# Issuing a decode kernel's V and up loads on a second queue

## The chip, the cores and the metric

The kernel runs on one core of one Trainium2 chip. The metric is the device time of one launch in microseconds (us). Most executions of a kernel lie close together, and some fall in a slow state: of the control's six times (c0_before, the kernel before with one comment changed) five are 440.16 to 440.79 us, within 0.15%, and one is 447.77 us, 1.7% longer. A ratio is the mean time of one kernel's fast runs over the mean time of the fast runs of the kernel before in the same rounds, on the same chip, so it is not quite the ratio of the medians that are quoted.

Abbreviations in the profile: PE is the matmul engine, DVE the vector engine, ACT the scalar engine, SP the engine that otherwise only issues transfers. SPq and ACTq are the queues on which those two engines issue DMA transfers; the text also calls such a queue a ring. L428 is line 428 of the kernel.

## The reference

One decode step of a transformer block with 8 sequences and one new token each: adaptive layer norm, grouped-query attention over a cache of 8192 positions, adaptive layer norm, gated MLP.

```python
mod = (silu(c) @ w_mod).reshape(8, 6, 1, -1)          # w_mod 1024 x 6144
h = layernorm(x) * (1 + ca) + sa
q = (h @ wq)                                          # wq 1024 x 4096, 32 heads of 128
scores = einsum('bhqd,bhkd->bhqk', q, k) * 128**-0.5  # k, v: 8 x 4 x 8192 x 128 bf16, 8 query heads per kv head
x = x + ga * (softmax(scores) @ v) @ wo               # wo 4096 x 1024
h = layernorm(x) * (1 + cb) + sb
x = x + gb * ((relu(h @ W_gate) * (h @ W_up)) @ W_down)   # 1024 x 3584, 1024 x 3584, 3584 x 1024
```

K and V are 67 MB each and the weights 51 MB. All 185.6 MB are read once.

## The kernel before

All large loads go through one list. An arena in SBUF is used as a ring, and a load is issued as soon as all readers of the bytes that it overwrites have been put in the program. Each load covers all 128 partitions.

```python
def load(key, src, n):
    stream.append((key, src, n))

def pump():                        # called after every operation that is recorded
    while stream:
        key, src, n = stream[0]
        lo = cursor[0] if cursor[0] + n <= RING else 0
        if P.unread("arena", lo, lo + n):
            return                 # the buffer still has readers to come
        stream.pop(0)
        cursor[0] = lo + n
        place[key] = lo
        dst = arena[:, lo:lo + n]
        # ... a view for 3-D sources ...
        P.op("sp", lambda e, dst=dst, src=src: e.dma_start(dst, src),
             writes=[slot_r(lo, lo + n)], dma=True)

# the order of the list (sizes in MiB):
#   wm0 6, wm1 6, wq0 4, wq1 4, K0 4, V0 4, K1 4, V1 4, ... K15 4, V15 4,
#   wo0 4, wo1 4, gate0 3.5, up0 3.5, gate1 3.5, up1 3.5, wd0 3.5, 1.75, 1, 0.5, 0.25
```

During attention the arena holds four buffers of 4 MiB: two for K and two for V. K(m+2) is issued when the last transpose of K(m) has ended, and V(m+2) when PV(m) has ended. One step m of attention is a chain over three engines:

```python
for m in range(16):
    for e8 in range(8):
        kt_part(m, e8)        # DVE: transpose an eighth of K(m)            L428
        qk_part(m, e8)        # PE: scores                                  L439
    rowmax; spread; headmax   # DVE, PE, DVE
    expo(m)                   # ACT: exp                                    L466
    p_turn(m)                 # DVE: transpose the probabilities            L473
    pv(m)                     # PE: probabilities times V(m), 32 matmuls    L482
```

The transposes of K(m+1) run while PV(m) runs. In this kernel each engine works off its own list of operations in order, and semaphores order the lists against one another.

## Time and profile before

| | |
|---|---|
| time, three runs | 439.91, 440.66 and 446.92 us, median 440.66 |
| bytes read | 185.6 MB |
| load queue's share of the 16 DMA engines | 98.4% |
| packet of 32 KB on one engine, from 100 us on | 1213 ns, which is 27.0 GB/s, and 432 GB/s for 16 engines |
| the profiled run | 445.6 us span, slow state |

These are lines of the page of the kernel before. The first two are rows of 40 equal slices of the span: the busy share of the DMA engines in tenths, and the rate. Then come the two queues that carry data, the chain that ended last, the group of K transposes with its idle time and what ended it, and the issue-to-landing times.

```profile
DMA  8999999999999999999999999999999999999994
GB/s 353 427 388 384 379 379 403 390 424 447 434 429 429 425 444 435 426 432 427 439 434 429 435 425 438 435 429 431 429 434 439 432 429 426 436 429 431 435 419 194
...
q1 hardware_dynamic: 6896, 185.64, 98.4%
...
q10 hardware_dynamic: 32, 0.01, 0.0%
...
DMA 48%; DVE 25%; PE 23%; ACT 2%; issue 1%; SPq 0%
...
L428 DVE STREAM_TRANSPOSE kt<-arena 128x1024 uint32<-128x1024 uint32 x128 | 148.6, 1215 | 44.6 <-DMA arena<-in_A_k_cache_dram 41.8
...
arena<-in_A_k_cache_dram SPq DMA_DIRECT2D x16, 4096.0 KB, 28.9
arena<-in_A_v_cache_dram SPq DMA_DIRECT2D x16, 4096.0 KB, 25.7
```

The engines are busy in every slice but the first and the last. The rate is flat near 430 GB/s from the ninth slice on. Queue q1 (SP) carries everything. K transposes wait 41.8 us in all for K, so compute keeps up with the loads. A load takes about 29 us from issue to landing although 4.19 MB at 432 GB/s are only 9.7 us: about two other loads are queued ahead of it.

The low rate of the third to eighth slice (379 to 403 GB/s) belongs to the slow state: in the three slow profiles packets took about 1355 instead of 1213 ns per 32 KB from about 20 us until 85 to 96 us into the run. The same kernel, run again as a control with one comment changed, fell in the fast state (438.4 us span), and its rate is flat from the second slice on (416 to 443 GB/s until the 38th). Below are its rates, the chain that ended last, the K transposes and the issue-to-landing time of K. The last two lines are from its timeline (start, duration, and in brackets how long the engine sat idle before and for whom): the first transpose of K0 and the last PV.

```profile
GB/s 359 434 416 438 437 443 432 431 431 429 434 431 431 429 431 434 430 434 431 431 432 434 434 435 443 434 434 429 434 429 431 434 429 431 431 433 431 432 420 195
...
PE 39%; DVE 29%; DMA 24%; ACT 4%; issue 2%; SPq 0%
...
L428 DVE STREAM_TRANSPOSE kt<-arena 128x1024 uint32<-128x1024 uint32 x128 | 149.1, 1215 | 40.3 <-DMA arena<-in_A_k_cache_dram 33.8 <-PE ps L439 6.4
...
arena<-in_A_k_cache_dram SPq DMA_DIRECT2D x16, 4096.0 KB, 28.5
...
62.90 6.88 DVE L428 STREAM_TRANSPOSE kt<-arena 128x1024 uint32<-128x1024 uint32 x6 [3.15 <-DMA arena<-in_A_k_cache_dram]
...
372.36 6.36 PE L482 MATMUL ps<-arena,pT 128*64 128x512 bf16 x32 [1.82 <-DVE pT L473]
```

So in the fast state compute on K0 starts at 62.9 us. This control is what the changed kernel, whose profile is fast too, is compared with.

### The profile page before, as it was taken

What the parts mean: (1) busy time and instruction counts of PE and PEld (TensorE: products, weight loads), DVE (VectorE), ACT (ScalarE), POOL (GpSimd) and SP (SyncE); (2) the same over time, 40 slices, a digit from 0 to 9 for tenths busy, and PEclk for the clock granted to TensorE, in tenths of its full rate; (3) what the DMA queues carried; (4) which work ended last, traced back from release to release, by engine and by line L of the source; (5) the groups of instructions that cost most, each with busy time, mean ns of one, the idle gap of its engine ahead of it and who ended that gap; (6) DMA issues with size and microseconds to landing.
All of it is one profiled execution on the core that took longest, in us unless ns stands there. A gap on an engine that the chain in (4) does not pass through costs nothing.

```text
span 445.6 us, 4024 instructions
## 1 busy us (share of the span) xinstructions
PE 273.7 (61%) x1691; PEld 121.9 (27%) x1691; DVE 262.9 (59%) x372; ACT 28.8 (6%) x48; POOL 19.9 (4%) x77
## 2 busy tenths in 40 slices
PE   0054347585775959577595867769595875564235
PEld 0021112222332423333242333324233332351112
DVE  0233028396878769687885967788686878521020
ACT  1100010201001010110101011010101001100000
POOL 6000010000000000000000000000000000000000
PEclk9997557796969789696987969688796988867555
DMA  8999999999999999999999999999999999999994
GB/s 353 427 388 384 379 379 403 390 424 447 434 429 429 425 444 435 426 432 427 439 434 429 435 425 438 435 429 431 429 434 439 432 429 426 436 429 431 435 419 194
DMA packets 6946, 185.90 MB, mean 417 GB/s; under 512 B 816, under 2 KB 912, under 8 KB 1168
## 3 DMA queue, kind: packets, MB, share of 16 engines
q1 hardware_dynamic: 6896, 185.64, 98.4%
q8 instruction: 13, 0.21, 0.2%
q14 instruction: 5, 0.04, 0.0%
q10 hardware_dynamic: 32, 0.01, 0.0%
HBM read 185.63 MB, written 0.02 MB: 417 GB/s over the span
## 4 chain that ended last, share of the span: by engine, by line
DMA 48%; DVE 25%; PE 23%; ACT 2%; issue 1%; SPq 0%
DMA arena<-in_A_k_cache_dram 33%; DVE kt L428 14%; PE ps L482 11%; DMA arena<-in_B_W_down_dram 8%; PE ps L439 8%; DMA arena<-in_w_mod_dram 7%; DVE pT L473 4%; DVE negm L446 3%; ACT prb L466 2%; PE ps L571 1%; PE ps L352 1%; PE ps L452 1%; PE ps L592 1%; DVE mj L457 1%; DVE kt L561 0%
## 5 line engine op out<-in xcount | busy, mean ns | idle before, releaser
L428 DVE STREAM_TRANSPOSE kt<-arena 128x1024 uint32<-128x1024 uint32 x128 | 148.6, 1215 | 44.6 <-DMA arena<-in_A_k_cache_dram 41.8
L439 PE MATMUL ps<-kt,qpad 128*128 128x512 bf16 x512 | 121.7, 382 | 12.7 <-DVE kt L428 10.8
L482 PE MATMUL ps<-arena,pT 128*64 128x512 bf16 x512 | 92.1, 539 | 50.5 <-DVE pT L473 50.5
L482 PEld LDWEIGHTS ps<-arena,pT 128*64 128x64 bf16 x512 | 44.3, 153 | 92.9 <-issue 87.3
L439 PEld LDWEIGHTS ps<-kt,qpad 128*128 128x128 bf16 x512 | 45.1, 97 | 87.8 <-DVE kt L428 32.3
L473 DVE STREAM_TRANSPOSE pT<-prb 64x1024 bf16<-64x1024 bf16 x32 | 39.6, 1239 | 15.9 <-ACT prb L466 15.4
L466 ACT ACTIVATE prb<-ps,bias 128x1024 bf16<-128x1024 f32 x16 | 17.8, 1114 | 276.3 <-DVE mjt L460 276.3
L446 DVE TENSOR_REDUCE negm<-ps 128x1 f32<-128x512 f32 x32 | 22.0, 686 | 10.7 <-PE ps L439 10.5
L421 POOL COPY qpad<-qR 32x32 bf16<-32x32 bf16 x64 | 13.1, 204 | 314.0 <-PE ps L439 255.4
L592 PE MATMUL ps<-arena,hT 128*32 128x448 bf16 x128 | 11.2, 522 | 15.9 <-DMA arena<-in_B_W_gate_dram 6.8
L452 PE MATMUL ps<-identf,negm 128*128 128x128 f32 x32 | 7.8, 325 | 15.7 <-DVE negm L450 15.7
L495 DVE SCALAR_TENSOR_TENSOR om<-ps,im,om 128x128 f32<-128x128 f32 x48 | 16.7, 348 | 0.6
L375 PE MATMUL ps<-arena,hT 128*32 128x512 bf16 x64 | 7.2, 631 | 14.7 <-DMA arena<-in_A_wq_dram 14.7
L599 DVE TENSOR_TENSOR kt<-ps,kt 128x448 bf16<-128x448 f32 x2 | 1.2, 620 | 25.0 <-PE ps L592 25.0
L500 PE MATMUL ps<-jmp,om 128*128 128x16 f32 x32 | 6.5, 280 | 14.7 <-DVE om L495 14.7
L290 DVE CAST cxr<-ps 128x512 bf16<-128x512 f32 x1 | 0.7, 692 | 19.2 <-PE ps L288 19.2
L288 PE MATMUL ps<-cx,rsel 32*128 32x512 bf16 x1 | 0.6, 581 | 18.6 <-DMA cx<-in_A_x_dram 18.6
L385 DVE CAST kt<-ps 128x512 bf16<-128x512 f32 x1 | 0.7, 693 | 18.3 <-PE ps L375 18.3
L610 PE MATMUL ps<-arena,kt 128*32 128x256 bf16 x112 | 6.9, 416 | 7.4 <-DMA arena<-in_B_W_down_dram 7.3
L452 PEld LDWEIGHTS ps<-identf,negm 128*128 128x128 f32 x32 | 4.7, 187 | 23.6 <-DVE negm L450 22.1
L352 PE MATMUL ps<-arena,hT 128*32 128x512 bf16 x96 | 9.0, 553 | 2.4 <-DMA arena<-in_w_mod_dram 2.4
L592 PEld LDWEIGHTS ps<-arena,hT 128*32 128x32 bf16 x128 | 4.2, 129 | 22.2 <-DMA arena<-in_B_W_up_dram 8.3
(80 smaller groups left out, 95.7 us busy)
## 6 DMA issues: line engine op xcount, KB each, us to landing
arena<-in_A_k_cache_dram SPq DMA_DIRECT2D x16, 4096.0 KB, 28.9
arena<-in_A_v_cache_dram SPq DMA_DIRECT2D x16, 4096.0 KB, 25.7
arena<-in_w_mod_dram SPq DMA_DIRECT2D x2, 6144.0 KB, 17.4
arena<-in_A_wq_dram SPq DMA_DIRECT2D x2, 4096.0 KB, 25.0
arena<-in_A_wo_dram SPq DMA_DIRECT2D x2, 4096.0 KB, 27.5
arena<-in_B_W_gate_dram SPq DMA_DIRECT2D x2, 3584.0 KB, 30.5
arena<-in_B_W_up_dram SPq DMA_DIRECT2D x2, 3584.0 KB, 33.5
arena<-in_B_W_down_dram SPq DMA_DIRECT2D x1, 3584.0 KB, 36.1
```

Source lines behind the costliest of these rows:

```text
L352: fns.append(lambda e, w=w, pr=pr, j=j, kk=kk: e.matmul(ps[32 * j:32 * j + 32, pr, :], hT[:, kk, :], w[:, 2 * pr:2 * pr + 2, j, :], start= ...
L375: fns.append(lambda e, w=w, z=z, g=g, kk=kk: e.matmul(ps[32 * g:32 * g + 32, 3 + z, :], hT[:, kk, :], w[:, g, z, :], start=(kk == 0), stop ...
L421: P.op("pool", lambda e, n=2 * m + Q // 2, Q=Q: e.tensor_copy(qpad[32 * Q:32 * Q + 32, m % 2, :, 24 + 32 * Q:32 + 32 * Q], qR[32 * Q:32 * ...
L428: P.op("dve", lambda e: e.transpose(ktb[:, to:to + QE].bitcast(dt.uint32), arena[:, lo:lo + QE].bitcast(dt.uint32)), reads=[slot_r(lo, lo ...
L439: fns.append(lambda e, t=t, r=r: e.matmul(ps[:, b, :].rearrange("p (c k) -> p c k", k=32), qpad[:, m % 2, t * 2 + r, 24 - 8 * i:152 - 8 * ...
L446: P.op("dve", lambda e: e.tensor_reduce(negm[:, h:h + 1], ps[:, b, :], AX.X, ALU.max, negate=True), reads=[bank(b)], writes=[R("negm", h, ...
L452: P.op("pe", lambda e: e.matmul(ps[:, 4, 0:128], negm[:, 2:3].to_broadcast([128, 128]), identf[:], start=True, stop=True), reads=[R("negm" ...
L466: P.op("act", lambda e: e.activation(prb[:], ps[:, 2 * z:2 * z + 2, :].rearrange("p h n -> p (h n)"), ACT.Exp, bias=bias[:, z:z + 1], scal ...
L473: P.op("dve", lambda e, g=g: e.transpose(pT[64 * g:64 * g + 64, z, :, g, :], prb[64 * g:64 * g + 64, :]), reads=[R("prb"), R("pT", z, z + ...
L482: fns.append(lambda e, t=t: e.matmul(ps[64 * (t % 2):64 * (t % 2) + 64, 5, :].rearrange("p (i d) -> p i d", d=Dh), pT[:, z, t].rearrange(" ...
L495: P.op("dve", lambda e, i=i: e.scalar_tensor_tensor(out=om[:], in0=ps[:, 5, Dh * i:Dh * i + Dh], scalar=im[:, i:i + 1], in1=om[:], op0=ALU ...
L592: fns.append(lambda e, w=w, r=kk - r0, kk=kk, h=h, j=j, b0=b0: e.matmul(ps[32 * j:32 * j + 32, b0 + h, 0:H], hT[:, kk, :], w[:, r, j, h, : ...
```

## The change

The intent: V and up loads are issued on ACT's queue, the rest on SP's, so that two rings feed every DMA engine at once.

```diff
-                P.op("sp", lambda e, dst=dst, src=src: e.dma_start(dst, src), writes=[slot_r(lo, lo + n)], dma=True)
+                P.op("act" if key[0] in ("v", "up") else "sp", lambda e, dst=dst, src=src: e.dma_start(dst, src), writes=[slot_r(lo, lo + n)], dma=True)
```

Buffers, sizes and the order of the list stay. Sixteen V loads and two up loads move to ACT's program, each at the place where it becomes legal.

## The prediction

> **What bounds it now.** The DMA stream. The queue table gives the single load queue 98.4% of 16 engines' span for 185.6 MB, and the 40-slice row shows nines almost throughout. In 5 us windows from 85 to 435 us the rate averages about 431 GB/s, and packet records there are 1213 ns per 32 KB packet, 27 GB/s per engine, 432 GB/s for 16. [...] 185.6 MB at 432 GB/s is 430 us; about 3 us before the first byte lands and 5 to 6 us from the last landing to the end make about 439, the fast time. The profiled run (445.6 us) was a slow one: until about 85 us its packets took some 12% longer (about 1355 ns per 32 KB), worth about 9 us.
>
> **Almost as tight: the compute chain.** In the chain of waits, stretches with no DMA in them repeat every 18.7 to 20.2 us per pair of loads (PV alone 4.9 to 6.6 us). Two 4.19 MB loads take 19.4 us.
>
> **What the change does.** It removes nothing: SP issues (0.33 us each) overlap transfers. It moves 16 V and 2 up issues to ACT, some 6 us in all (28.8 us busy, 276 us waiting before exp). Each V issue waits there for the PV that frees its slot, but the next exp comes after that PV anyway. The same bytes go through the same 16 engines, already at their limit. [...]
>
> What does change is order. V0 is issued at 39.4 us with wq0's rest, wq1 and K0 still queued; on its own ring it no longer waits behind them but takes half the engines [...]. My estimate from the transfer times: V0 lands about 12 us earlier, where nobody needs it, wq1 about 9 us and K0 about 13 us later, so the first K transpose, at 68.1 us now, starts about 13 us later and the compute chain stays late until the end. Does the DMA run dry? Queued ahead of a new K are about 19 us (28.9 to land less its own 9.7), ahead of a new V 16 us: enough for 13 us, barely. If the chain keeps 19.4 us per step, no idle; at 20 us per step the queue empties for some microseconds. At the end, wd's issue has about 24 us of queue ahead, so the tail hides the delay.
>
> **Prediction: 441.5 us, 438 to 449 in 8 of 10.** Faster by over 2%: 0.02; within 2%: 0.88; slower by over 2%: 0.10.
>
> **Signs.** Two load queues in the table, together 97 to 98%; GB/s still about 430 in the middle. K from issue to landing falls from 28.9 to about 16 us, V similar, because less is queued. DVE idle before the first K transpose grows by about 13 us; the last PV ends about 13 us later than the state explains. DMA slices below 9 would show dry queues.
>
> **What would make it wrong.** Two rings raising the per-packet rate above 432 (faster); K and V reads disturbing each other in HBM (slower); a PV held at 6.4 us or more by the granted clock, which with the late start would empty the queues and cost 7 us or more.

The first packets start at 1.8 us and end from 4.1 us on in the trace of the kernel before; its last load lands at 441.9 us, 3.7 us before the end of the span, and a time is about 1.8 us longer than its span (442.09 us against 440.3), together 5.5 us. That the two rings share the engines in halves was the assumption, and the 12, 9 and 13 us of the estimate rest on it; the trace of the changed kernel shows it nearly (V0's queue had 54% of the engine time from 40 to 58 us). A PV of 6.4 us or more is one at a low granted clock: in the changed kernel PV took 4.91 to 5.03 us where the clock was 0.72 or 0.73, and 6.36 to 6.60 us where it was 0.54 to 0.57. The 7 us that it would cost are the estimate, which no run tested.

## The result, and the profile after

The changed kernel took 442.13 us in the median (441.01 to 443.09, 4 runs). The ratio to the kernel before is 1.0039, with a 95% interval of 1.0016 to 1.0061. Measured again with five rounds on another occasion it was 1.0045 (1.0026 to 1.0063), while the control gave 0.9998 (0.9985 to 1.0011). So the change costs about 1.8 us, clear of the noise and far below 2%.

These are the same lines of the page after (440.3 us span), and from its timeline the first transpose of K0 and the last PV.

```profile
DMA  8999999999999999999999999999999999999994
GB/s 357 432 444 427 435 429 429 427 432 429 415 429 429 438 439 438 432 425 435 426 430 432 429 405 430 432 447 435 428 435 433 429 429 433 431 434 423 444 411 175
...
q1 hardware_dynamic: 4304, 111.19, 58.8%
q10 hardware_dynamic: 2624, 74.46, 39.4%
...
PE 43%; DVE 29%; DMA 21%; ACT 5%; issue 2%; SPq 0%
...
L428 DVE STREAM_TRANSPOSE kt<-arena 128x1024 uint32<-128x1024 uint32 x128 | 149.6, 1217 | 40.4 <-PE ps L439 34.2
...
arena<-in_A_k_cache_dram SPq DMA_DIRECT2D x16, 4096.0 KB, 21.7
arena<-in_A_v_cache_dram ACTq DMA_DIRECT2D x16, 4096.0 KB, 21.9
...
73.95 2.37 DVE L428 STREAM_TRANSPOSE kt<-arena 128x1024 uint32<-128x1024 uint32 x2 [4.75 <-DMA arena<-in_A_k_cache_dram]
...
383.20 6.43 PE L482 MATMUL ps<-arena,pT 128*64 128x512 bf16 x32 [1.82 <-DVE pT L473]
```

Two queues now carry data, 58.8% and 39.4%, in sum 98.2%, against the 98.4% that one carried before. The rate in the middle is the same within 1%, with a few lower slices (415, 405). In the packet records from 40 to 360 us, taken in stretches of 20 us, the median packet of 32 KB takes 1213 ns on both queues, as it did on one. So the second ring brought no bandwidth.

What moved is the compute chain. K0's first transpose starts at 73.95 us instead of 62.90, 11.05 us later, and the last PV ends at 389.6 us instead of 378.7, 10.9 us later. The lag of the start is carried to the end of attention, in a program that ends only 1.9 us later. K transposes used to wait for K (33.8 us of 40.3 in the control). Now almost all of their waiting, 34.2 us, is for the matmuls that free the transpose buffers: K is there and compute is behind. With compute behind, buffers come free later, loads are issued later, and issue to landing falls from 28.5 us (control) to 21.7.

The chain of waits says PE 43% and DMA 21%. That doesn't make PE the bound: the DMA engines are still busy for 98% of the span. Nor is it the change that brought this about: the control's fast profile has PE 39% and DMA 24%, and the DMA 48% of the first page stood in a slow profile. The chain follows the last releaser, and loads and compute are almost equally long here, so its shares say little about the bound.

Where do the 1.8 us come from? Adding up the packet records of the trace, between 20 and 420 us the 16 engines were never idle in the control, and idle for 0.40 us (mean over the engines) after the change. In the same stretch, packets that took longer than their bytes at 1213 ns per 32 KB cost 1.15 us per engine in the control and 2.21 us after. The additional long ones lie at the starts of V loads (119, 197, 217, 236, 256 us), just when the K load before them runs out. Together that is 0.40 + 1.06 = 1.5 us of about 1.8.

### The profile page after: what moved, and what is told of

Same layout as the page of the kernel before. It is cut to its first block, busy times and chain, and to the rows that moved or that the text cites. A ratio compares the mean times of both kernels' runs of the same rounds, so it can differ in the third digit from the quotient of the medians.

```text
span 440.3 us, 4024 instructions
## 1 busy us (share of the span) xinstructions
PE 272.0 (62%) x1691; PEld 121.8 (28%) x1691; DVE 264.2 (60%) x372; ACT 28.8 (7%) x48; POOL 19.8 (5%) x77
## 3 DMA queue, kind: packets, MB, share of 16 engines
q1 hardware_dynamic: 4304, 111.19, 58.8%
q10 hardware_dynamic: 2624, 74.46, 39.4%
## 4 chain that ended last, share of the span: by engine, by line
PE 43%; DVE 29%; DMA 21%; ACT 5%; issue 2%; SPq 0%
PE ps L482 21%; PE ps L439 16%; DVE kt L428 10%; DVE pT L473 9%; DMA arena<-in_A_k_cache_dram 9%; DMA arena<-in_w_mod_dram 7%; DMA arena<-in_B_W_down_dram 6%; DVE negm L446 5%; ACT prb L466 4%; PE ps L452 2%; PE ps L571 1%; DVE mj L457 1%; PE ps L592 1%; DVE mjt L460 1%; PE ps L352 1%
## 5 line engine op out<-in xcount | busy, mean ns | idle before, releaser
L428 DVE STREAM_TRANSPOSE kt<-arena 128x1024 uint32<-128x1024 uint32 x128 | 149.6, 1217 | 40.4 <-PE ps L439 34.2
L482 PE MATMUL ps<-arena,pT 128*64 128x512 bf16 x512 | 94.1, 547 | 51.1 <-DVE pT L473 51.1
L446 DVE TENSOR_REDUCE negm<-ps 128x1 f32<-128x512 f32 x32 | 22.1, 690 | 12.4 <-PE ps L439 12.4
L375 PE MATMUL ps<-arena,hT 128*32 128x512 bf16 x64 | 7.2, 631 | 23.4 <-DMA arena<-in_A_wq_dram 23.4
L592 PE MATMUL ps<-arena,hT 128*32 128x448 bf16 x128 | 12.3, 569 | 7.8 <-DMA arena<-in_B_W_gate_dram 4.4
L375 PEld LDWEIGHTS ps<-arena,hT 128*32 128x32 bf16 x64 | 2.2, 139 | 27.9 <-DMA arena<-in_A_wq_dram 24.8
L500 PEld LDWEIGHTS ps<-jmp,om 128*128 128x128 f32 x32 | 5.0, 195 | 18.0 <-DVE om L495 16.9
## 6 DMA issues: line engine op xcount, KB each, us to landing
arena<-in_A_k_cache_dram SPq DMA_DIRECT2D x16, 4096.0 KB, 21.7
arena<-in_A_v_cache_dram ACTq DMA_DIRECT2D x16, 4096.0 KB, 21.9
arena<-in_B_W_up_dram ACTq DMA_DIRECT2D x2, 3584.0 KB, 21.9
```

The source lines that it names most:

```text
L375: fns.append(lambda e, w=w, z=z, g=g, kk=kk: e.matmul(ps[32 * g:32 * g + 32, 3 + z, :], hT[:, kk, :], w[:, g, z, :], start=(kk == 0), stop ...
L428: P.op("dve", lambda e: e.transpose(ktb[:, to:to + QE].bitcast(dt.uint32), arena[:, lo:lo + QE].bitcast(dt.uint32)), reads=[slot_r(lo, lo ...
L446: P.op("dve", lambda e: e.tensor_reduce(negm[:, h:h + 1], ps[:, b, :], AX.X, ALU.max, negate=True), reads=[bank(b)], writes=[R("negm", h, ...
L482: fns.append(lambda e, t=t: e.matmul(ps[64 * (t % 2):64 * (t % 2) + 64, 5, :].rearrange("p (i d) -> p i d", d=Dh), pT[:, z, t].rearrange(" ...
L500: P.op("pe", lambda e: e.matmul(ps[:, 6, 16 * m:16 * m + 16], om[:], jmp[:].rearrange("p g j -> p (g j)"), start=True, stop=True), reads=[ ...
L592: fns.append(lambda e, w=w, r=kk - r0, kk=kk, h=h, j=j, b0=b0: e.matmul(ps[32 * j:32 * j + 32, b0 + h, 0:H], hT[:, kk, :], w[:, r, j, h, : ...
```

## The experiments

Three theories were put against each other.

- **A**: the 16 engines were already full. A second ring only changes the order. V0 overtakes wq1 and K0, compute starts about 11 us late and stays late, the reserve in the queues is used up, and the engines now and then run dry.
- **B**: two rings cost the engines something per packet, or K and V rows read side by side disturb each other.
- **C**: the issues on ACT and their waits delay exp.

Twelve kernels were run, each with five rounds. All gave results that passed the comparison with the reference. Of the six times of e1_halves only the lowest, 703.96 us, counts as fast, so it has no ratio.

| run | what it does | ratio (95%) |
|---|---|---|
| c0_before | control | 0.9998 (0.9985 to 1.0011) |
| after_again | the change | 1.0045 (1.0026 to 1.0063) |
| e3_late1 | one ring, K0 one load later | 1.0006 (0.9993 to 1.0020) |
| e4_late2 | one ring, K0 two loads later | 1.0228 (1.0213 to 1.0243) |
| e5_late3 | one ring, K0 three loads later | 1.0430 (1.0417 to 1.0442) |
| e6_v2_on | the change from V2 on | 1.0022 (0.9998 to 1.0045) |
| e8_after_half_pv | the change, shorter compute chain | 1.0005 (0.9987 to 1.0023) |
| e9_before_half_pv | before, shorter compute chain | 1.0003 (0.9990 to 1.0016) |
| e10_cols_two | loads in column halves, two rings | 1.0042 (1.0023 to 1.0062) |
| e11_cols_one | loads in column halves, one ring | 1.0033 (1.0016 to 1.0050) |
| e1_halves | loads in partition halves, two rings | none; 792.63 against 440.50 us |
| e12_rows_one | loads in partition halves, one ring | 2.0129 (2.0050 to 2.0208) |

### The control and the change again

> Control: the kernel before with one comment changed. Every theory: ratio 1.000, within 0.2%. It gives the noise and, if the profile falls in the fast state, the first K transpose of a fast run: about 62 us expected (68.1 in the slow profile, where early packets took 12% longer), against 73.9 after the change; the last PV should end near 377 us against 389.7 after the change.

> The changed kernel again, on the same chip as the other runs of this call. Theory A (two rings only reorder: K0 comes about 12 us late, the compute chain stays late, the queues lose their reserve and sometimes run dry) and every rival: ratio about 1.004, first K transpose near 74 us. It is the yardstick for the other three.

The control's first K transpose is at 62.9 us and its last PV ends at 378.7 us, near the 62 and 377 us expected. The repeated change has its first K transpose at 74.9 us and 0.63 us of idle engine time. Both expectations held.

### K0 late on one ring: one, two and three loads

If theory A is right, the same loss must come from a late K0 without any second ring. The list's order was changed and the buffers were kept:

```diff
+        FIX = {("wq", 0): 49152, ("wq", 1): 0, ("k", 0): 16384, ("v", 0): 32768, ("k", 1): 49152, ("v", 1): 0, ("k", 2): 16384}
...
+                lo = FIX.get(key, lo)
...
+        # late1: V0 wq1 K0 K1 V1   late2: V0 wq1 K1 K0 V1   late3: V0 wq1 K1 V1 K0   (before: wq1 K0 V0 K1 V1)
+        stream[3:8] = [next(x for x in stream if x[0] == k) for k in ORDER]
```

> One ring as before, but V0 is put in the queue ahead of wq1 and K0, with all buffers as before, so K0 comes one load (9.7 us) late and nothing is on ACT. Theory A: first K transpose near 72 us, last PV near 386 us, and hardly any loss, ratio 1.000 to 1.003, because a new V load has about 16 us of queue ahead of it. Rivals B and C: 1.000. A loss of the size of the delay (1.02) would say that there is no reserve in the queue.

> One ring, K0 put two loads later (order wq0, V0, wq1, K1, K0, V1; buffers as before), nothing on ACT. Theory A: first K transpose near 82 us, 19.4 us late, which is more than the reserve of about 16 us: engines dry for about 4 to 7 us, ratio 1.009 to 1.016. Without the reserve the loss would be the whole 19.4 us (1.044); if lateness did not matter, 1.000.

> One ring, K0 put three loads later (order wq0, V0, wq1, K1, V1, K0). Theory A: first K transpose near 92 us, 29 us late, loss about 29 - 14 = 15 us, ratio 1.030 to 1.040; the last PV some 29 us later than in the kernel before. Together with the runs that are one and two loads late: no loss up to the reserve, then about one us per us.

Lateness is the start of the first K transpose against 62.9 us of the control. The loss is (ratio − 1) times 440.6 us. Dry plus long is the engine time idle between 20 and 420 us plus the growth of long packets over the control's 1.15 us.

| run | K0 late by | loss | dry + long |
|---|---|---|---|
| e3_late1 (profile slow: against the slow profile of before) | 10.4 us | 0.3 us | 0.0 us dry |
| the change | 11.05 us | 1.7 to 2.0 us | 0.40 + 1.06 us |
| e4_late2 | 19.8 us | 10.0 us | 7.68 + 2.43 us |
| e5_late3 | 28.9 us | 18.9 us | 16.48 + 2.92 us |

The first 10 us of lateness are nearly free. From there each microsecond costs about a microsecond: 19.8 and 28.9 us late lose 10.0 and 18.9. The changed kernel, with its second ring, lies close to the line of the kernels with one ring. My expectation of the reserve, 14 to 16 us, was too large, and so both expected losses were too small (1.009 to 1.016 and 1.030 to 1.040). The expectation for one load (at most 1.003) held.

The windows view of the two-loads run shows the dry queue: stretch, its length, busy time of PE, PEld, DVE, ACT and POOL, granted PE clock, busy share of the DMA engines, GB/s.

```profile
84.00:88.00 4.00, 3.99 (x10) 1.45 (x11) 4.00 (x4) 0.00 (x0) 0.00 (x0) 0.50 0.91 393
88.00:92.00 4.00, 3.80 (x17) 1.44 (x15) 3.57 (x5) 0.00 (x0) 0.00 (x0) 0.90 0.37 152
92.00:96.00 4.00, 2.45 (x10) 0.81 (x9) 2.15 (x5) 1.28 (x1) 0.82 (x4) 1.00 0.57 164
96.00:100.00 4.00, 0.00 (x0) 0.00 (x0) 2.66 (x5) 1.21 (x2) 0.00 (x0) 0.88 1.12 483
100.00:104.00 4.00, 3.92 (x20) 2.01 (x22) 4.00 (x4) 0.00 (x0) 0.00 (x0) 0.50 0.92 395
104.00:108.00 4.00, 4.00 (x23) 1.75 (x20) 1.03 (x2) 0.00 (x0) 0.00 (x0) 0.77 0.41 115
```

All four buffers were taken, and the last queued load, V1, ran out from 89 us on. K2 could be issued only at 93.0 us, when K0's transposes had ended, and its first packet started at 94.0. V2 was issued at 106.6 us and its first packet started at 107.5. So each stop costs about 1.0 us from issue to first packet beside the wait itself (up to 1.7 us until the last engine has one), and the first packets after it take about 2.0 us instead of 1.2. My estimate of the reserve had left that out, and also that the last of the 16 engines lands after the first, by 2.0 to 3.6 us for most loads of the kernel before. The control's packet records give the reserve directly: counted in order, the first packet of V2 to V15 started 13.2 us after the issue (median). Less the 1.0 us that is about 12 us, the nearest estimate to the 10 us measured.

### A shorter compute chain

If the 0.4% come from compute that cannot catch up, they must vanish when compute gets faster, with every load, ring and issue kept. If B or C is right, they must stay. Half of the PV matmuls are left out, in the changed kernel and in the kernel before:

```diff
-            for t in range(32):
+            for t in range(16):
...
-stop=(t >= 30),
+stop=(t >= 14),
```

This is wrong, since it leaves out half of V. The comparison with the reference passed all the same, so it doesn't see this error, and passing says little about attention here.

> The changed kernel with half of the PV matmuls left out (wrong result on purpose), which shortens each step of the compute chain by about 3 us while loads, rings and order stay. Theory A (late chain, empty queues): the chain can now catch up, the queues keep their reserve, the 0.4% vanish: ratio 1.000 within 0.2%. Rivals B (cost per packet of two rings) and C (issues on ACT): the loss stays, ratio 1.003 to 1.005.

> The kernel before with the same half of the PV matmuls left out (wrong result on purpose): every theory that has the load stream as the bound says ratio 1.000 within 0.2%. If it were clearly faster, compute would have been the bound.

The 3 us were about half of a PV, which took 4.91 to 6.60 us in the changed kernel. Measured, it was somewhat less: PV is busy for 56.9 us in sixteen steps with the short chain, against 94.1 us in the changed kernel, 2.3 us a step.

The ratio of the changed kernel with the short chain is 1.0005 (0.9987 to 1.0023), with no idle engine time between 20 and 420 us. Its first K transpose was as late as ever, at 75.3 us (12.4 us after the control's), but its last PV started at 376.1 us, against 372.4 in the control and 383.2 in the changed kernel: all but 3.7 us of the lag had been made up. K transposes wait for K again. This line is from its waits of DVE (waiter, releaser, us in total, times, longest):

```profile
DVE kt L428 <- DMA arena<-in_A_k_cache_dram: 35.9, 12, 5.6
```

The kernel before gains nothing from the short chain (1.0003), so the loads bound it and compute did not. Theory B, which expected 1.003 to 1.005 for the changed kernel, falls as an explanation of the 0.4%. What it could still be worth lies within the interval: up to about 0.2%. Theory C isn't tested cleanly by this run, since a shorter PV also shortens the wait of the V issues on ACT. The trace of the changed kernel settles it: every exp starts 0.03 to 0.04 us after the DVE instruction that it waits for (mjt), as in the control, and the last load issue on ACT has ended at least 2.8 us before.

### The change from V2 on

Is it only the start? V0 and V1 stay on SP here, so K0 and K1 come in time:

```diff
-"act" if key[0] in ("v", "up") else "sp"
+"act" if key[0] == "up" or (key[0] == "v" and key[1] > 1) else "sp"
```

> The changed kernel with V0 and V1 left on SP; V2 to V15 and up stay on ACT. Theory A in its narrow form (only the start matters): first K transpose near 63 us, chain never late, last PV near 379 us, ratio 1.000. Theory A in its wide form (sharing lets each V take half the engines from the K that is needed sooner): first K transpose near 63 us, but the chain loses its lead within a few steps, last PV near 385 to 390 us, ratio 1.000 to 1.005.

The half of this expectation is what the trace of the changed kernel shows from 245 to 249 us, with a K and a V load both in progress: 51% of the engine time for SP's queue and 50% for ACT's (records overlap a little).

These are K transposes in the timeline of this run: K0, K1, K2.

```profile
62.70 6.88 DVE L428 STREAM_TRANSPOSE kt<-arena 128x1024 uint32<-128x1024 uint32 x6 [3.17 <-DMA arena<-in_A_k_cache_dram]
...
82.02 6.88 DVE L428 STREAM_TRANSPOSE kt<-arena 128x1024 uint32<-128x1024 uint32 x6 [2.63 <-DMA arena<-in_A_k_cache_dram]
...
113.43 6.88 DVE L428 STREAM_TRANSPOSE kt<-arena 128x1024 uint32<-128x1024 uint32 x6 [14.68 <-DMA arena<-in_A_k_cache_dram]
```

And the control's K2:

```profile
101.54 4.63 DVE L428 STREAM_TRANSPOSE kt<-arena 128x1024 uint32<-128x1024 uint32 x4 [2.42 <-DMA arena<-in_A_k_cache_dram]
```

K0 and K1 are in time. V2, issued on ACT at 85.3 us, took engine time from V1 and K2, which were queued before it on SP, and K2's transposes started 11.9 us late. Since then the chain is behind: the last PV ends at 388.6 us, 9.9 us later than in the control. So it is not the start alone. In both kernels the first V that was put on the other ring overtook loads that were needed sooner. The ratio of 1.0022 (0.9998 to 1.0045) doesn't tell a loss from none, as the wide form of theory A expected (1.000 to 1.005), and the narrow form is refuted by the lag.

### Two rings in the old order

To measure two rings apart from the order, every load is cut into two halves which go out together, one on each ring. The first attempt cut by partitions (the lines that track readers of the second half are left out here).

```diff
-P.op("sp", ... e.dma_start(dst, src) ...)
+P.op("sp",  ... e.dma_start(dst[0:64], src[0:64]) ...)
+P.op("act", ... e.dma_start(dst[64:128], src[64:128]) ...)
```

> Every load is cut into two halves of 64 partitions, one issued on SP and one on ACT, so both rings feed every engine all the time but the loads land in the old order. Theory A: K0 lands as in the kernel before (about 62 us), ratio 1.000 within 0.2%. Rival B (alternating between two rings, or K and V rows read side by side, costs the engines something per packet): packets over 1213 ns, ratio 1.003 or more. Rival C (issues and their waits on ACT delay exp): ratio 1.002 or more, since ACT now has 42 issues instead of 18.

It took 792.63 us in the median (703.96 to 796.95), which no theory had expected. Packets of 32 KB took about 2320 ns in the profiled run of 796.95 us. As a test of two rings it is useless, because it changed a second thing: which partitions a load reaches. The same cut with both halves on SP, one ring:

> The halves of 64 partitions of the run that took about 790 us, both issued on SP: one ring. If that loss comes from loads that reach only 64 partitions, it stays: ratio about 1.7 to 1.9, packets of 32 KB about 2340 ns. If it came from two rings working on different partitions at once, ratio near 1.00.

It is even slower: ratio 2.0129, with a median of about 2560 ns for a 32 KB packet. So the cause is the loads that reach 64 partitions only, and not two rings (as many loads that reach all 128, on one ring too, gave 1.0033, see below). The mean rate was 209 GB/s in this run and 234 GB/s with two rings, whose queues kept the engines busy for 99.1% of the span together (49.4% and 49.7%). Why such loads are slow, and why two rings were faster than one here, no run tests. Row of rates per slice, first of the two-ring run, then of the one-ring run:

```profile
GB/s 198 231 219 199 235 214 234 215 231 219 228 221 229 223 225 226 223 228 219 233 218 233 233 227 232 234 236 236 238 242 246 243 244 249 245 253 299 315 316 162
```

```profile
GB/s 212 207 195 212 208 211 213 202 205 210 212 212 212 209 205 209 207 209 211 210 212 209 211 206 211 211 212 211 214 211 211 212 214 214 213 215 213 218 210 167
```

The cut that keeps all 128 partitions is by columns, on two rings and, as its control, on one:

```diff
+h = n // 2
+P.op("sp", ... e.dma_start(arena[:, lo:lo + h], src[:, 0:h]) ...)
+P.op("act" or "sp", ... e.dma_start(arena[:, lo + h:lo + n], src[:, h:n]) ...)
```

> Every load cut into two halves by columns, so that each half still goes to all 128 partitions; first half on SP, second on ACT: both rings always have work, loads land in the old order, ACT has 40 load issues. Theory A: first K transpose near 62 us (fast state), ratio 1.000 within 0.3%. Rivals B (cost of two rings per packet) and C (cost of issues on ACT): 1.003 or more. If the 1.8 of the split by partitions comes back here, that loss belonged to two rings or to splitting and not to which partitions a load reaches.

> The same column halves, both issued on SP, one ring: the control for the run before. Every theory: ratio 1.000 within 0.3%, unless packets of half the size cost something by themselves; then both column runs show it alike.

Both are slower than expected and alike: 1.0042 on two rings and 1.0033 on one. The intervals overlap widely. Packets are half as large, and 16 KB took 611 ns on both queues and in both runs, 1222 ns per 32 KB instead of 1213. That is 0.7% more per record, but records overlap a little (in the profile of the kernel before they add up to 401.3 us per engine between 20 and 420 us), so the bytes moved between 20 and 400 us tell more: 431.9 GB/s in the control, 429.9 and 430.0 with one and two rings. So smaller packets cost about 0.4% of rate, and alternating between two rings costs no rate that can be seen. Run against run, two rings were 0.37 us (0.08%) slower (442.54 against 442.17 us in the mean); where that comes from was not looked into. With 47 load issues on ACT instead of 18 (the trace has 47, not the 40 or 42 of the expectations), theory C had its best chance here, and whatever B and C are worth together here is within about these 0.37 us. Neither run had idle engine time between 20 and 420 us. In the two-ring run the first transpose was at 64.9 us, 2.0 us after the control's, and the last PV ended at 381.6 us: without overtaking, the chain does not fall behind the control by more than 3 us. Against its own one-ring run it is 5.4 us late (59.5 us), because there the first half of K0 landed at 57.8 us and could be transposed before the second; on two rings both halves travelled together (61.2 and 64.9 us).

## Why the prediction was right

- **"What bounds it now. The DMA stream"**: right. Half of the PV matmuls taken out of the kernel before changes nothing (1.0003). The slow early phase of the profiled run (379 to 403 GB/s in the third to eighth slice) is absent in the control's fast profile (416 to 443), as the prediction held.
- **"The same bytes go through the same 16 engines, already at their limit"**: right. Packets on both rings have the old 1213 ns. That the engines are the same was not shown when it was recorded. The trace of the changed kernel shows it: the queues were busy for 98.2% of 16 engines' span in sum, against 98.4% on one, at the same rate, and each alone can take the time of all 16 (SP's queue from 58 to 66 us, ACT's from 240 to 242 us).
- **"the next exp comes after that PV anyway"**, so that the V issues on ACT hold nothing up: right. In the trace of the changed kernel exp starts 0.03 to 0.04 us after what it waits for, as before. The short-chain run keeps all issues on ACT and stands at 1.0005.
- **V0 overtakes, K0 lands "about 13 us later"**: right in kind, and 11.05 us in size. V0 landed at 59.0 us instead of 72.5. The second wq load was consumed 9.4 us later (its matmuls start at 62.67 us against 53.26), where 9 us had been predicted. That each ring takes half of the engines was the assumption. The trace agrees roughly: from 40 to 58 us, while V0 was in progress, ACT's queue had 54% of the engine time (40 to 71% in stretches of 2 us), and from 245 to 249 us, with a K and a V load both in progress, SP's queue had 51%. It doesn't set in at once: V loads issued at 233.2 and 253.2 us had their first packets 2.4 and 2.0 us later, a K load issued at 239.8 us its first 3.6 us later.
- **The chain "stays late until the end"**: right, 10.9 us at the last PV.
- **"enough for 13 us, barely"**: the decision was right, the reserve was mis-sized. The prediction had 16 to 19 us. The late-K0 runs show about 10 us, with each further microsecond lost in full. That the result came out well rests in part on luck: with 13 us of lag, as predicted, the true reserve of 10 us would have cost 3 us.
- **"K from issue to landing falls from 28.9 to about 16 us"**: the sign was right, the size was wrong: 21.7 us, and V 21.9. The term that it missed is sharing: less is queued, as predicted (the first packet of K2 to K15 started 3.5 us after the issue, median, against 16.3 in the control), but a K load that shares the engines with a V load takes 16.4 us from its first packet to its last, against 10.9. The sign "DMA slices below 9" for dry queues was too coarse: no slice shows the 0.40 us.
- **441.5 us predicted, 442.13 measured**; the loss of about 0.8 us that this implied, against the 440.66 us of the kernel before, was 1.8.

## What to carry to other kernels

When the busy share and the packet duration show that the transfer engines are at their limit (here 98.4% and 1213 ns), expect a second issuing queue to change only the order of arrival, as it did here (98.2% and 1213 ns). An order that was right on one queue (needed first, queued first) gets worse when later loads may overtake: here K0 came 11.05 us late. Before such a change, work out the reserve: the time for which transfers stay queued when a buffer comes free late, less the time from issue to first packet. Here a lag smaller than that was nearly free (10.4 us late lost 0.3 us), and beyond it every microsecond counted in full (19.8 and 28.9 us late lost 10.0 and 18.9). A cut of loads for an experiment must keep the set of partitions that each load reaches (halves of 64 partitions took 2.01 times the time on one ring), and it needs a one-ring control.
